# The first head's top-k mask from VectorE to ScalarE, for 27 of 36 query tiles

## The chip, the cores and the metric

One core of a Trainium2 chip runs one program. TensorE (PE in the rows) multiplies matrices, VectorE (DVE), ScalarE (ACT) and GpSimd (POOL) work elementwise, SyncE (SP) issues most DMAs. Each engine executes its own instructions in order and waits at semaphores for the others. The metric is the device time of one execution in microseconds (us).

## What is computed

Attention that keeps the 32 largest scores of each row, then a layer of four gated experts, then a layer that takes the largest of three products, all in float32:

```python
scores = scale * np.matmul(q, k.transpose(0, 1, 3, 2))     # 2 batches, 8 heads, 576 x 64
kth = np.partition(scores, -top_k, axis=-1)[..., -top_k:-top_k + 1]
mask = scores >= kth
scores = np.where(mask, scores, -1000000000.0)
attn = np.exp(scores - np.max(scores, axis=-1, keepdims=True))
attn = attn / (np.sum(attn, axis=-1, keepdims=True) + 1e-09)
x = np.matmul(attn, v)                                     # -> 1152 x 512
...
out += p[:, e:e + 1] * (np.maximum(x @ w1[e], 0.0) @ w2[e])      # 4 experts, 512 -> 1024 -> 512
...
h = np.maximum(np.maximum(x @ w1, x @ w2), x @ w3)               # 512 -> 768
return h @ w_out
```

## The kernel before, in words

**Units of work.** The 1152 rows are nine tiles of 128, in four chunks of 2, 2, 2 and 3 tiles. Attention runs over 36 *pairs*: a pair is one row tile and two heads, j = 0 (the first) and j = 1. Pairs are numbered from 0 here; the change concerns pairs 9 to 35. The layers after attention run by *phases*: experts of chunk 0, 1, 2, 3, then the last layer in three groups of tiles. The experts of a chunk need all of the chunk's attention. Each float32 product is three matmuls on split operands (high part and rest), at lines 606 to 608.

**One pair.** TensorE makes the scores (L368, bank `pss`), ScalarE copies them to `s` (L376). VectorE finds the 32 largest in seven steps, four of MAX8 (L389) and three of MATCH_REPLACE8 (L391), so that the last column of `m` is the 32nd largest, `kth`. ScalarE negates the maximum (`nb`, L396) and writes `p` = exp(SCALE s + nb) (L402). The *mask* then keeps of `p` what belongs to a score that is at least `kth`, and adds it up into `rs`: on VectorE one SCALAR_TENSOR_TENSOR with an accumulator (L409); the very first pairs do it on GpSimd. TensorE transposes the masked `p` (L427, and L432 for the last 64 columns of both heads), ScalarE copies that to `pt` (L430, L435), TensorE multiplies by v (`psv`, L469 and L472). On the side go the sum's guard (`rs`, L440), its reciprocal `rr` on VectorE (L446), its spreading `rb` on ScalarE (L450), a transpose `psr` (L455) and the copy `r` (L457); `xt` (L479) is the normalised tile.

**What sets the order.** The program is written out slot by slot, eight slots a pair. Each step of a pair stands at a fixed slot from the pair's first. For pairs 8 and later (table LOOSE) the second head runs 4 slots behind the first; the mask stands 7 slots after a head's first MAX8, the transposes 9 slots after it, their copies two slots later, the guard, reciprocal and spreading at slots 13, 14 and 15 of the pair, the product with v at 16. In between a planner puts the products of the layers (and the weight splits that they need, L229 and L235): it counts VectorE's work in a clock of its own (`dve`, 0.07 + n/960 us for n columns, a mask too) and TensorE's in another (`pe`), and after each slot issues products until TensorE's count has caught up with VectorE's.

```python
two(b0 + 7, pr.mask, j, lag=o["sum"] if n < EARLY else 3)
two(b0 + o["trans"], pr.trans_p, j)
...
clock["goal"] += (clock["dve"] - before) * SHARE[min(phase[0], len(SHARE) - 1)]
while clock["pe"] < clock["goal"]:
    if not advance():
```

The tiles of normalised attention are kept as `x`, in two sets that alternate between chunks. The `x` of chunk 3 takes the place of that of chunk 1, so it can only be written once the experts of chunk 1 are issued (`x_free`); tiles that come earlier wait in a list, `waiting`. After attention 48 pieces of the last layer's weights are converted (L200 to L212), and the remaining products follow.

Of the kernel before, what the change touches and what calls it, by code (L numbers as in the profile page):

```python
# [10 lines left out]
F32 = mybir.dt.float32  # L11
# [3 lines left out]
AF = mybir.ActivationFunctionType  # L15
# [11 lines left out]
PAUSE = 0.8  # L27
LATE = 3
ON_POOL = ((0, 1, 2, 3, 4, 5, 6, 7), (0, 1, 2, 3, 4, 5, 6))
W_FIRST, W_AHEAD = 60, 4  # L30
WIDE, W_FROM, W_STEP = 4, 306, 2

# [19 lines left out]
def kernel(  # L52
# [276 lines left out]
    def advance():  # L329

        return next(work, "end") not in (None, "end")
# [17 lines left out]
    class Pair:  # L349
        def __init__(self, n):  # L350
            self.c, self.hp, self.t = pairs[n]
            self.s, self.w, self.m, self.nb = {}, {}, {}, {}
            self.p = self.rs = None
            self.pt = {}

            self.did = set()

            self.on_pool = [n in ON_POOL[j] for j in range(2)]

        def scores(self, j):  # L360
            srcs = [(b, i) for i, (t, b) in enumerate(SLOTS[self.c]) if t == self.t]
# [36 lines left out]
        def exp(self, j):  # L398
            if self.p is None:
                self.p = at.tile([P, 2, S], F32, tag="p", name="p")  # L400
                self.rs = at.tile([P, 2], F32, tag="rs", bufs=3, name="rs")
            nc.scalar.activation(out=self.p[:, j].rearrange("p (a n) -> p a n", a=2), in_=self.s[j], func=AF.Exp, bias=self.nb[j], scale=SCALE)  # L402

        def mask(self, j):
            p = self.p[:, j].rearrange("p (a n) -> p a n", a=2)
            s, kth, total = self.s[j], self.m[j][:, TOPK - 1:TOPK], self.rs[:, j:j + 1]
            if not self.on_pool[j]:
                dve(S)
                nc.vector.scalar_tensor_tensor(out=p, in0=s, scalar=kth, in1=p, op0=ALU.is_ge, op1=ALU.mult, accum_out=total)  # L409
                self.did.update([("p", j), ("sum", j)])  # L410
                return lambda: None
            nc.gpsimd.tensor_scalar(out=s, in0=s, scalar1=kth, scalar2=None, op0=ALU.is_ge)
            nc.gpsimd.tensor_tensor(out=p, in0=p, in1=s, op=ALU.mult)  # L413
            self.did.add(("p", j))

            def add():
                nc.scalar.activation(out=s, in_=p, func=AF.Copy, accum_out=total)
                self.did.add(("sum", j))
            return add
# [74 lines left out]
    def attention():  # L494
# [34 lines left out]
        for n, (c, hp, t) in enumerate(pairs):  # L529
            s0 = 8 * n  # L530
            prs[n] = Pair(n)
            pr = prs[n]
            o = options(n)

            def two(s, f, *a, lag=o["lag"]):
                at_slot(s, lambda: at_slot(s + lag, f(*a)))
            for j in range(2):
                b0 = s0 + o["stag"] * j
                two(b0 + o["scores"], pr.scores, j)
                for i in range(7):  # L540
                    if o["new"]:
                        later.setdefault(b0 + i, []).insert(0, (pr.topk, (j, i)))
                    else:
                        at_slot(b0 + i, pr.topk, j, i)
                at_slot(b0 + 2, pr.negate, j)
                at_slot(b0 + 5, pr.exp, j)
                two(b0 + 7, pr.mask, j, lag=o["sum"] if n < EARLY else 3)
                two(b0 + o["trans"], pr.trans_p, j)
            two(s0 + o["stag"] + o["trans"], pr.trans_p, 2)
            at_slot(s0 + o["rec"] - 1, pr.guard)  # L550
            at_slot(s0 + o["rec"], pr.recip)
            at_slot(s0 + o["rec"] + 1, pr.spread)
            at_slot(s0 + o["pv"], pr.pv)
            two(s0 + o["rec"] + 2, pr.trans_r)
            end = max(o["pv"], o["rec"] + 2) + o["lag"]
            at_slot(s0 + end + 1, pr.norm)
            two(s0 + end + 2, pr.split_x)
# [282 lines left out]
    for s, done in attention():  # L840
        if s == GATES:
            load_gates()
        if s == GATES + 26:
            norm_gates()
        if s == W_FIRST - 12:
            w_load_to(3)
        if W_FIRST <= s < W_FIRST + 16 and not (s - W_FIRST) % 4:
            w_split_to((s - W_FIRST) // 4 + 1)
        if s == W_FROM - 6:
            for i in range(AHEAD_S):  # L850
                wide_load(i)
        if s >= W_FROM + W_STEP * conv and conv < WIDE * len(wide):
            converting.append(to_float32(conv))
            conv += 1
        for x in list(converting):
            if next(x, 0) == 0:
                converting.remove(x)
        split_waiting()
        assert not any((x.c, x.hp) in done for x in waiting)
        x_ready.update(done)  # L860
        clock["goal"] += (clock["dve"] - before) * SHARE[min(phase[0], len(SHARE) - 1)]
        before = clock["dve"]
        while clock["pe"] < clock["goal"]:
            if not advance():
                clock["pe"] = clock["goal"]
# [67 lines left out]
```

## Time and profile before

| | before |
|---|---|
| median of 3 runs | 778.3 us (776.51 to 778.96) |
| profiled execution, its own time | 778.73 us |
| its span on the engines | 776.9 us |
| TensorE / VectorE / ScalarE / GpSimd busy | 93% / 85% / 62% / 70% of the span |

The span runs from the first to the last instruction; the own time holds 1.8 us more around it. Busy shares are means over a program with three parts: attention alone (to about 100 us), attention with the experts' products in between (to about 471 us, when the last mask is done), and products with the conversion of weights. Durations of neighbouring matmuls overlap in the rows, so the price of one is the distance from its start to the next start, not its duration.

### The profile page before, as it was taken

How to read it: one execution, taken by the hardware profiler on the slowest of the kernel's cores; microseconds unless marked ns; L12 is line 12 of the kernel's file. 1: busy time of each engine (PE TensorE's matmuls, PEld its weight loads, DVE VectorE, ACT ScalarE, POOL GpSimd, SP SyncE). 2: the span in 40 equal slices, each digit the busy share in tenths (PEclk: the TensorE clock that was granted, in tenths of full speed). 3: DMA queues.
4: the chain of work that ended last, by engine and by line, in shares of the span. 5: the costliest groups of instructions: out<-in, count | busy, mean ns of one | idle time of the engine just before them, and what ended most of it. 6: DMA issues, size and time to landing. Idle time of an engine off the chain costs nothing. (4 is left out here: it accounts for less than half of the span.)

```text
span 776.9 us, 13519 instructions
## 1 busy us (share of the span) xinstructions
PE 725.2 (93%) x4646; PEld 655.3 (84%) x4646; DVE 659.9 (85%) x1247; ACT 482.3 (62%) x1021; POOL 541.4 (70%) x440
## 2 busy tenths in 40 slices
PE   3666799999999999998999998999999999999998
PEld 2545689988998988887998997989998799899996
DVE  6999999999999999999999996898899994243341
ACT  5666768767786876766777675655565643342441
POOL 3887988889998878778878695675677673343430
PEclk9986699999999999999999999999999999999999
DMA  4430255466645446263554454977667864362421
GB/s 117 105 111 1 60 147 162 137 179 163 195 142 177 126 148 180 87 180 107 150 145 137 137 163 153 301 233 250 221 215 260 252 204 136 102 211 92 156 91 40
DMA packets 48612, 119.91 MB, mean 154 GB/s; under 512 B 7840, under 2 KB 18080, under 8 KB 48544
## 3 DMA queue, kind: packets, MB, share of 16 engines
q1 hardware_dynamic: 40336, 110.40, 46.6%
q10 hardware_dynamic: 8208, 8.65, 3.2%
q8 instruction: 36, 0.59, 0.3%
q14 instruction: 32, 0.26, 0.1%
HBM read 110.38 MB, written 8.65 MB: 153 GB/s over the span
## 5 line engine op out<-in xcount | busy, mean ns | idle before, releaser
L235 POOL TENSOR_TENSOR wlo<-raw,whi 128x512 fp32r<-128x512 f32 x260 | 359.7, 1413 | 129.8 <-ACT whi L229 128.9
L229 ACT ACTIVATE whi<-raw 128x1024 fp32r<-128x1024 f32 x164 | 170.3, 1057 | 41.1 <-DMA raw<-in_w_dram 16.7
L389 DVE MAX8 m<-work 128x8 f32<-128x576 f32 x216 | 154.1, 739 | 0.1
L606 PE MATMUL ps<-xl,whi 128*128 128x256 f32 (+1 forms) x512 | 153.6, 300 | 0.0
L608 PE MATMUL ps<-xh,wlo 128*128 128x256 f32 (+1 forms) x512 | 151.3, 296 | 0.0
L607 PE MATMUL ps<-xh,whi 128*128 128x256 f32 (+1 forms) x512 | 151.2, 295 | 0.0
L235 DVE TENSOR_TENSOR wlo<-raw,whi 128x1024 fp32r<-128x1024 f32 x34 | 52.7, 1550 | 67.2 <-ACT whi L229 55.9
L391 DVE MATCH_REPLACE8 work<-m,work 128x576 f32<-128x576 f32 x144 | 106.0, 736 | 0.0
L607 PEld LDWEIGHTS ps<-xh,whi 128*128 128x128 f32 x512 | 97.2, 190 | 0.9
L606 PEld LDWEIGHTS ps<-xl,whi 128*128 128x128 f32 x512 | 97.1, 190 | 1.0
L608 PEld LDWEIGHTS ps<-xh,wlo 128*128 128x128 f32 x512 | 97.1, 190 | 0.0
L606 PE MATMUL ps<-wlo,h 128*128 128x512 f32 x192 | 77.6, 404 | 0.0
L608 PE MATMUL ps<-whi,h 128*128 128x512 f32 x192 | 75.4, 392 | 0.0
L607 PE MATMUL ps<-whi,h 128*128 128x512 f32 x192 | 75.3, 392 | 0.0
L409 DVE SCALAR_TENSOR_TENSOR p<-s,m,p 128x576 f32<-128x576 f32 x57 | 73.8, 1295 | 0.0
L608 PE MATMUL ps<-x2h,wlo 128*128 128x384 f32 x216 | 72.8, 337 | 0.0
L606 PE MATMUL ps<-x2l,whi 128*128 128x384 f32 x216 | 72.7, 337 | 0.0
L607 PE MATMUL ps<-x2h,whi 128*128 128x384 f32 x216 | 72.6, 336 | 0.0
L368 PE MATMUL pss<-kT,ql 128*128 128x288 f32 x160 | 54.7, 356 | 14.1 <-DVE ql L312 7.5
L212 POOL TENSOR_TENSOR narrow<-narrow,raw 128x256 int32<-128x256 int32 x48 | 40.3, 840 | 39.3 <-DVE narrow L209 10.5
L427 PE MATMUL psp<-ident,p 128*128 128x128 f32 x288 | 49.1, 298 | 17.8 <-POOL p L413 11.9
L427 PEld LDWEIGHTS psp<-ident,p 128*128 128x128 f32 x288 | 37.3, 153 | 24.4 <-POOL p L413 15.5
(97 smaller groups left out, 1632.6 us busy)
## 6 DMA issues: line engine op xcount, KB each, us to landing
raw<-in_w_dram SPq DMA_DIRECT2D x128, 512.0 KB, 3.7
raw<-narrow SPq DMA_DIRECT2D x36, 512.0 KB, 3.4
raw<-in_m_dram SPq DMA_DIRECT2D x36, 256.0 KB, 4.9
narrow<-narrow ACTq DMA_DIRECT2D x48, 128.0 KB, 4.4
kraw<-in_k_dram SPq DMA_DIRECT2D x14, 288.0 KB, 4.5
raw<-in_mo_dram SPq DMA_DIRECT2D x12, 256.0 KB, 4.3
out_dram<-ob ACTq DMA_DIRECT2D x9, 256.0 KB, 2.0
vt<-in_v_dram SPq DMA_DIRECT2D x8, 256.0 KB, 3.7
```

The lines of the kernel that those rows point to most:

```text
L212: nc.gpsimd.tensor_tensor(out=out.bitcast(I32), in0=out.bitcast(I32), in1=last, op=ALU.add)
L229: nc.scalar.activation(out=hi, in_=raw, func=AF.Copy)
L235: on.tensor_tensor(out=lo[:, x], in0=raw[:, x], in1=hi[:, x].bitcast(F32), op=ALU.subtract)
L368: nc.tensor.matmul(ps[:, 0:SH], lhsT=l, rhs=r, start=i == 0, stop=i == len(mm) - 1)
L389: nc.vector.max(m[:, 8 * r:8 * r + 8], src)
L391: nc.vector.match_replace(out=self.w[j], in_to_replace=m[:, 8 * r:8 * r + 8], in_values=src, imm_value=NEG)
L409: nc.vector.scalar_tensor_tensor(out=p, in0=s, scalar=kth, in1=p, op0=ALU.is_ge, op1=ALU.mult, accum_out=total)
L427: nc.tensor.transpose(ps[:, r * P:(r + 1) * P], self.p[:, part, part * TAIL + r * P:part * TAIL + (r + 1) * P], ident)
L606: nc.tensor.matmul(ps, lhsT=lh, rhs=rl, start=first, stop=False)
L607: nc.tensor.matmul(ps, lhsT=lh, rhs=rh, start=False, stop=False)
L608: nc.tensor.matmul(ps, lhsT=ll, rhs=rh, start=False, stop=last)
```

## The change

For head j = 0 of pairs 9 to 35 (27 masks) the mask goes from VectorE to ScalarE, as three activations. The first writes max(kth - s, 0) + 2^-100 min(kth - s, 0) over the scores `s` (a parametric ReLU). The second makes a bias of one column, `eb` = SCALE kth + nb. The third is exp(-SCALE 2^100 s + eb) into `p`, with the sum in its accumulator: a score below `kth` gives exp of a huge negative number, 0, and one that is at least `kth` gives exp(SCALE s + nb) as before. The old exponential of that head goes. The mask of these heads stands two slots later, and the transposes of the masked `p` three slots later. VectorE's count no longer holds these masks. Where the slots' end of a chunk finds a tile that still waits for `x`, products are now issued until it has its place.

```diff
+ON_ACT = (range(9, 36), ())
+STEEP = 2.0 ** 100
+MASK_LATE = 2
...
+            self.on_act = [n in ON_ACT[j] for j in range(2)]
...
-            nc.scalar.activation(out=self.p[:, j].rearrange("p (a n) -> p a n", a=2), in_=self.s[j], func=AF.Exp, bias=self.nb[j], scale=SCALE)
+            if not self.on_act[j]:
+                nc.scalar.activation(out=self.p[:, j].rearrange("p (a n) -> p a n", a=2), in_=self.s[j], func=AF.Exp, bias=self.nb[j], scale=SCALE)
...
+            if self.on_act[j]:
+                eb = at.tile([P, 1], F32, tag="eb%d" % j, name="eb")
+                nc.scalar.activation(out=s, in_=s, func=AF.Prelu, scale=-1.0, bias=kth, alpha=1.0 / STEEP)
+                nc.scalar.activation(out=eb, in_=kth, func=AF.Identity, scale=SCALE, bias=self.nb[j])
+                nc.scalar.activation(out=p, in_=s, func=AF.Exp, scale=-SCALE * STEEP, bias=eb, accum_out=total)
+                self.did.update([("p", j), ("sum", j)])
+                return lambda: None
...
-                two(b0 + 7, pr.mask, j, lag=o["sum"] if n < EARLY else 3)
-                two(b0 + o["trans"], pr.trans_p, j)
+                late = MASK_LATE * pr.on_act[j]
+                two(b0 + 7 + late, pr.mask, j, lag=o["sum"] if n < EARLY else 3)
+                two(b0 + o["trans"] + late + (late > 0), pr.trans_p, j)
...
-        assert not any((x.c, x.hp) in done for x in waiting)
+        while any((x.c, x.hp) in done for x in waiting):
+            assert advance()
+            clock["goal"] = max(clock["goal"], clock["pe"])
+            split_waiting()
```

How this stands in the built programs. VectorE, in the middle of attention, over about a pair, before (the two L409 rows are the masks of one head each):

```order
L409 SCALAR_TENSOR_TENSOR p,rs<-s,m_3192,p 128x576
L389 MAX m_3375<-s 128x8
L389 MAX m_3293<-work 128x8
L391 MATCH_REPLACE work<-m_3375,s 128x576
L391 MATCH_REPLACE work<-m_3293,work 128x576
L389 MAX m_3375<-work 128x8
L389 MAX m_3293<-work 128x8
L686 SCALAR_TENSOR_TENSOR h<-ps_3260,h 128x512
L391 MATCH_REPLACE work<-m_3375,work 128x576
L479 TENSOR_TENSOR xt<-psv,r 128x128
L409 SCALAR_TENSOR_TENSOR p,rs<-s,m_3293,p 128x576
```

The same half of a pair on VectorE in the changed program, whose lines are numbered 4 to 12 higher:

```order
L458 RECIPROCAL rr<-rs 128x2
L395 MATCH_REPLACE work<-m_3224,work 128x576
L393 MAX m_3313<-s 128x8
L393 MAX m_3224<-work 128x8
L395 MATCH_REPLACE work<-m_3313,s 128x576
L395 MATCH_REPLACE work<-m_3224,work 128x576
L393 MAX m_3313<-work 128x8
L393 MAX m_3224<-work 128x8
L395 MATCH_REPLACE work<-m_3313,work 128x576
L491 TENSOR_TENSOR xt<-psv,r 128x128
L421 SCALAR_TENSOR_TENSOR p,rs<-s,m_3224,p 128x576
```

After the reciprocal the search of the next head starts at once: only the second head's mask is left.

ScalarE at the same place, before: the tail of one pair (`rb`, two `pt`) runs into the exponentials of the next.

```order
L396 ACTIVATE nb<-m_3638 128x1
L376 ACTIVATE s<-pss 128x288 x2
L678 ACTIVATE h<-raw 128x512
L450 ACTIVATE rb<-rr 128x128
L430 ACTIVATE pt<-psp 128x512
L435 ACTIVATE pt_3666<-psp 128x128
L229 ACTIVATE whi<-raw 128x1024
L684 ACTIVATE h<-ps_3685 128x512
L402 ACTIVATE p<-s,nb 128x576
L396 ACTIVATE nb<-m_3750 128x1
```

And in the changed program:

```order
L442 ACTIVATE pt<-psp 128x512
L380 ACTIVATE s<-pss 128x288 x2
L232 ACTIVATE whi<-raw 128x1024
L697 ACTIVATE h<-ps_3567 128x512
L462 ACTIVATE rb<-rr 128x128
L442 ACTIVATE pt<-psp 128x512
L447 ACTIVATE pt_3609<-psp 128x128
L414 ACTIVATE s<-s,m_3482 128x576
L415 ACTIVATE eb<-m_3482,nb 128x1
L416 ACTIVATE p,rs<-s,eb 128x576
L407 ACTIVATE p<-s,nb 128x576
L232 ACTIVATE whi<-raw 128x1024
```

Three new activations stand in one block behind the copies of the pair before, and the first head's `pt` copy has moved down to just ahead of the second's.

TensorE around pair 28, from its last transposes to its product with v, in the changed program (matmuls of the layers between them left out):

```order
L439 MATMUL psp<-ident,p 128x128 x4
L372 MATMUL pss<-kT,ql 128x288
...
L439 MATMUL psp<-ident,p 128x128 x4
L444 MATMUL psp<-ident,p 128x128
L619 MATMUL ps_4627<-wlo,h 128x512
...
L621 MATMUL ps_4840<-xh,wlo 128x256
L481 MATMUL psv<-pt_4668,v_last_115 128x128
L484 MATMUL psv<-pt,vt 64x128 x8
```

In the dots after the L444 row stand 102 matmuls of the layers; at the same pair before there were 48. It is the place where the added loop issues products so that chunk 3 gets its `x`. By the last pair's transposes the program before has issued 1152 of the layers' matmuls of 256 columns and 534 of 512, the changed one 1104 and 516; the rest comes later.

## Rows read from the trace of the kernel before

**Rows 1.** page, part 1 (busy us, share, instructions) and TensorE's slices of part 2

```profile
PE 725.2 (93%) x4646; PEld 655.3 (84%) x4646; DVE 659.9 (85%) x1247; ACT 482.3 (62%) x1021; POOL 541.4 (70%) x440
...
PE   3666799999999999998999998999999999999998
```

**Rows 2.** busy time by stretch, to and from the last mask at 471

```profile
110.00:471.00 361.00, 352.77 (x2660) 318.85 (x2658) 360.38 (x743) 265.09 (x571) 304.30 (x241) 1.00 0.52 153
471.00:776.90 305.90, 300.66 (x1581) 277.23 (x1579) 196.46 (x282) 145.90 (x261) 155.87 (x128) 1.00 0.56 181
```

**Rows 3.** waits of VectorE, 110 to 471 us: total, times, longest

```profile
DVE rr L446 <- ACT rs L440: 0.3, 1, 0.3
```

**Rows 4.** matmuls by line and shape, 110 to 471 us

```profile
L606 PE MATMUL ps<-xl,whi 128*128 128x256 f32 x354 | 102.1, 288 | 0.0
...
L606 PE MATMUL ps<-wlo,h 128*128 128x512 f32 x178 | 72.1, 405 | 0.0
```

**Rows 5.** TensorE's timeline, neighbours of 256 and 512 columns: start, us

```profile
294.95 0.39 PE L608 MATMUL ps<-whi,h 128*128 128x512 f32 x1
295.18 0.40 PE L606 MATMUL ps<-wlo,h 128*128 128x512 f32 x1
...
303.03 0.28 PE L607 MATMUL ps<-xh,whi 128*128 128x256 f32 x1
303.15 0.28 PE L608 MATMUL ps<-xh,wlo 128*128 128x256 f32 x1
```

**Rows 6.** TensorE's timeline, an attention pair's own matmuls

```profile
311.24 0.29 PE L368 MATMUL pss<-kT,ql 128*128 128x288 f32 x1
311.37 0.29 PE L368 MATMUL pss<-kT,qh 128*128 128x288 f32 x1
...
313.17 0.60 PE L427 MATMUL psp<-ident,p 128*128 128x128 f32 x4
313.60 0.27 PE L432 MATMUL psp<-ident,p 128*128 128x128 f32 x1
...
316.48 0.38 PE L469 MATMUL psv<-pt,v_last 128*128 128x128 f32 x2
...
317.90 0.38 PE L368 MATMUL pss<-kT,ql 128*128 128x288 f32 x1
```

**Rows 7.** groups of instructions, whole span: busy us, mean ns of one

```profile
L402 ACT ACTIVATE p<-s,nb 128x576 f32<-128x576 f32 x72 | 55.7, 774 | 0.0
...
L409 DVE SCALAR_TENSOR_TENSOR p<-s,m,p 128x576 f32<-128x576 f32 x57 | 73.8, 1295 | 0.0
...
L396 ACT ACTIVATE nb<-m 128x1 f32<-128x1 f32 x72 | 14.0, 197 | 10.5 <-DVE m L389 10.3
...
L409 DVE DVE_READ_ACCUMULATOR p<-s,m,p 128x1 f32 x57 | 4.3, 76 | 0.0
...
L417 ACT ACTIVATION_READ_ACCUMULATOR s<-p 128x1 f32 x15 | 2.8, 187 | 0.0
...
L106 ACT ACT_TABLE_LOAD x1 | 1.3, 1283 | 0.7 <-PEq L912 0.7
```

**Rows 8.** line 409's durations: min/median/max ns, first and last start

```profile
L409 DVE SCALAR_TENSOR_TENSOR p<-s,m,p x57: 797/1321/1948, 92.0 to 469.5; 128x576 f32<-128x576 f32 x57
```

**Rows 9.** VectorE's timeline, two of these masks

```profile
309.42 1.29 DVE L409 SCALAR_TENSOR_TENSOR p<-s,m,p 128x576 f32<-128x576 f32 x1
...
315.53 0.80 DVE L409 SCALAR_TENSOR_TENSOR p<-s,m,p 128x576 f32<-128x576 f32 x1
```

**Rows 10.** GpSimd's timeline at these masks

```profile
308.80 3.08 POOL L235 TENSOR_TENSOR wlo<-raw,whi 128x512 fp32r<-128x512 f32 x2 [1.29 <-ACT whi L229]
...
317.57 5.67 POOL L235 TENSOR_TENSOR wlo<-raw,whi 128x512 fp32r<-128x512 f32 x4 [5.28 <-ACT whi L229]
```

**Rows 11.** waits of ScalarE, 110 to 471 us

```profile
ACT rb L450 <- DVE rr L446: 27.5, 20, 2.6
```

**Rows 12.** waits of TensorE, 110 to 471 us

```profile
PE psv L469 <- ACT pt L435: 3.5, 4, 1.6
```

## The prediction

> **What bounds the kernel now.** First the busy shares and the slices: TensorE is at 9 tenths or more in nearly every slice from a seventh of the span on, VectorE averages 85% [rows 1]. Two engines can be full at once, so the next view is the busy time by stretch. The change touches pairs 9 to 35, and these lie between 110 and 471 us. There VectorE is busy for 360.38 of 361.00 us, TensorE for 352.77, GpSimd for 304.30 and ScalarE for 265.09; behind 471 us TensorE has 300.66 of 305.90 and VectorE only 196.46 [rows 2]. The waits say which of the two paces attention: VectorE waited 0.3 us in 361, once [rows 3]. So attention runs as fast as VectorE does, and what follows runs as fast as TensorE does.
>
> The gain is not what VectorE saves. TensorE has a fixed amount of work, and from the first products to the end it is nearly always at it; the program can only become shorter by the time in which TensorE does nothing. How much is that between 110 and 471? Two bounds. What the busy time leaves open is 361.00 - 352.77 = 8.2 us [rows 2]; the ends of matmuls are modelled there, so short waits can hide. The other bound counts. There are 3 x 354 matmuls of the layers with 256 columns and 3 x 178 with 512 (lines 606, 607 and 608 alike) [rows 4]. Where nothing holds them up, their starts are 0.12 and 0.23 us apart [rows 5]: 1062 x 0.12 + 534 x 0.23 = 127.4 + 122.8 = 250.2 us. A pair's own matmuls: eight for the scores at 0.13 (1.04), eight transposes in two groups at 0.43 and the small one at 0.1 (0.96), the product with v and `psr` 317.90 - 316.48 = 1.42 [rows 6]; together 3.42, times 27 is 92.3. 361 - 250.2 - 92.3 = 18.5 us. This end is too high: four of the 27 pairs cover a tile with rows of both batches and take more. I take 12 us of idle, nearer to the end that is read directly, with 8.2 and 18.5 kept for the range.
>
> **The change part by part.**
>
> *VectorE.* 27 masks go, each 1.295 + 0.076 us with its accumulator read [rows 7]: 37.0 us. The mean hides two prices: the quickest mask took 0.797 us, the slowest 1.948 [rows 8]. The mask at 309.42 us took 1.29 us while GpSimd was in a subtraction; that at 315.53 took 0.80, and GpSimd stood idle then until 317.57 [rows 9, 10]. The removed masks stand where the kept ones do, so the mean holds for them too. If no GpSimd work met them, it would be 27 x 0.873 = 23.6 us. VectorE alone would end attention at 471 - 37.0 = 434 us (447 by the other price).
>
> *TensorE.* No matmul is added, but the planner lets products through as its count of VectorE's work grows, and that count loses the 27 masks. By the last pair's transposes the changed program has issued 48 fewer matmuls of 256 columns and 18 fewer of 512: 48 x 0.12 + 18 x 0.23 = 9.9 us [rows 5] that move behind attention, where TensorE is the pace. So the part behind attention grows from 305.9 to 315.8 us. TensorE's need up to there is 361 - 12 - 9.9 = 339.1 us; without any idle it would come to the last pair at 449.1 us. VectorE could be there at 434. TensorE becomes the pace of this part too, and 449.1 + 315.8 = 764.9 us is the least that the span can be with 12 us of idle at stake.
>
> *ScalarE.* The old exponential (0.774) is replaced by one with an accumulator (0.774, and 0.187 for the read), and there are two more: the parametric ReLU over the same 576 columns and a bias of one column. Neither occurs in the rows. The nearest to the first is the exponential, with a column as its bias as well, 0.774; a copy of one column takes 0.197 [rows 7]. Below, the ReLU can't be less than the 0.187 of a read; above, I allow the two 1.3 us together for their waits on each other, since each reads what the one ahead wrote. I take 0.774 + 0.197 + 0.187 = 1.16 us a mask, 31.3 us (between 15 and 40). 265.1 + 31.3 = 296.4 us in about 343 us is 86%, where it was 73%. This hides as long as ScalarE's waits shrink: it had 95.9 us without work [rows 2] and would have 47. 27.5 us of them were waits of `rb` for VectorE's reciprocal, 20 times [rows 11], and these go as VectorE stops being late.
>
> *Later mask, later transposes.* Two slots later for `p`, three for its transposes: the product with v is still at slot 16, so the first head's `pt` copy now stands right ahead of the second's. TensorE waits for these copies already, 3.5 us in 4 waits [rows 12]. Behind the waiting `psv` on TensorE stand `psr`, the next scores and products. The copies wait behind `rb`, which waits for VectorE; with VectorE ahead of TensorE this wait becomes shorter, while a fuller ScalarE makes it longer. I let these cancel.
>
> *The forced products.* At pair 28 TensorE gets 102 products in place of 48 ahead of the next pairs' scores: 54 x 0.23 = 12.4 us at most [rows 5]. TensorE is working in that time, so this costs it nothing. VectorE may stand still for as much, and its time for attention is then 434 + 12.4 = 446 us, still below 449. If the masks' price is the low one it is 459, ten past 449, and the span 459 + 315.8 = 774.8, the upper end of the forecast's own range.
>
> *Hidden.* GpSimd loses what TensorE's postponed products would have asked of it and gains nothing; the new `eb` tile and the longer life of `s` meet no reader on the path.
>
> **The sum.** 776.9 - 12 of TensorE's idle, + 4 us that stay: a third of the present, because TensorE and VectorE now want nearly the same time per pair (339 and 324 us for 27) and must meet several times in each. Span 768.9; with 1.8 around it 770.7. The profiled run's own time, 778.73, is 0.4 above the median, so the median would be 770.3: **770 us**, 1.1% less.
>
> **Rivals.**
>
> *A, the forecast:* TensorE paces attention, 8 to 18.5 us of idle less what stays: 761 to 775. Chance 0.63.
>
> *B, ScalarE becomes the pace, slower.* Its waits belong to its order and need not vanish: it stops at `rb`, `r`, `xt` and scores whatever its load, and a block of three activations (about 2 us) now stands ahead of the second head's exponential and the next score copies. If all 95.9 us stayed, attention would take 361 + 31.3 us and the program 110 + 392.3 + 315.8 = 818 us. It breaks even where attention ends at 461, which allows 351 - 296.4 = 54.6 us, 57% of the waits. With three quarters staying, 71.9 us, it is 110 + 368.3 + 315.8 = 794. For it: 86% load in strict order. Against it: VectorE's single wait of 0.3 us shows that ScalarE has been well ahead of it. Chance 0.20.
>
> *C, nothing to gain.* TensorE's idle is only the visible 8.2 us, and waits for late `pt` copies make up for them: 776 to 780. For it: those copies now come three in a row. Chance 0.15.
>
> *E, table switches.* ScalarE loaded its table once, 1.283 us [rows 7]; if the new functions asked for another table twice a mask, 54 x 1.283 = 69 us would be added to ScalarE, 365 us without a single wait, and the program would take at least 110 + 365 + 315.8 = 791 us. The changed program holds one load, at its start, as before, which speaks against it. Chance 0.02. The Trainium skill (ScalarE: Activation LUTs, Table sets: the hidden batching unit) advises to batch activations by table set and not by function. Its figure of about 2.66 us a switch would make 144 us of the 54. No row here shows a second load.
>
> **Range and chances.** Of A, 761 and above; upward it takes in all of C and the part of B that is near break-even: **761 to 783 us**, which leaves out nearly all the rest of B, E and a sliver of A below 761, 2 in 10 together. A alone: 761 to 775. Changes under 0.3%, 2.3 us, can't be told from none in this kernel. Faster by more (below 776): A and a little of C, 0.65. Within: most of C and B's edge, 0.15. Slower: 0.20.
>
> **What the changed profile would show.** Right: attention's last mask at about 453 us in place of 471; VectorE with tens of us of waits where it had 0.3, mostly for scores or products, one long one near pair 28; TensorE's busy time closer to its stretch; 27 parametric ReLUs near 0.77 us; ScalarE near 86% of attention, its wait at `rb` far below 27.5 us. Wrong: if TensorE waits for `psv` or `psp` more than now, with ScalarE as the releaser, B or C holds; if the last mask is at 471 or later, B. If VectorE still has no waits, its masks were worth less than 37 us, or TensorE's idle was larger than 12.

## The result: 785.98 us, slower by 1%

Four runs of the changed kernel took 785.28 to 788.04 us, median 785.98; the kernel before had 778.63 beside them. The ratio is 1.0100 [1.0067, 1.0133]: slower, outside the range of 761 to 783. The profiled execution took 785.28 us with a span of 783.5. The page of the changed kernel, where [rows 1] stood before:

```profile
PE 726.8 (93%) x4646; PEld 657.8 (84%) x4646; DVE 638.6 (82%) x1193; ACT 504.5 (64%) x1102; POOL 530.5 (68%) x440
...
PE   3665799999996999999999998999999999999998
```

TensorE has a 6 in a stretch that was full, the thirteenth slice (235 to 255 us). The second view is the end of attention. The last mask of VectorE (line 421; durations, then the starts of the first and the last of the two masks in the window):

```profile
L421 DVE SCALAR_TENSOR_TENSOR p<-s,m,p x2: 1482/1512/1541, 450.6 to 461.7; 128x576 f32<-128x576 f32 x2
```

It ends at 463.1 us. Before, it ended at 470.3 (the 471 of [rows 2] is the round end of a stretch), and the prediction had 453. The busy time on both sides of it, where [rows 2] stood before (span, then busy us of PE, PEld, DVE, ACT, POOL, granted clock, DMA share, GB/s):

```profile
110.00:463.10 353.10, 343.99 (x2600) 312.12 (x2598) 329.50 (x688) 282.69 (x646) 283.39 (x234) 0.99 0.51 149
463.10:783.50 320.40, 312.08 (x1650) 287.04 (x1650) 207.89 (x289) 151.50 (x269) 167.24 (x135) 0.99 0.56 181
```

VectorE, which had 0.6 us without work in its stretch, now has 23.6. But TensorE has not closed up: 9.1 us are open where 8.2 were. Behind the last mask the program takes 320.4 us, 4.6 more than the forecast 315.8. So the loss against the forecast has two parts, 10.1 us in attention and 4.6 behind it; together, but for rounding, the span's 783.5 against the forecast 768.9.

The new instructions on ScalarE, by group (busy us, mean ns of one):

```profile
L414 ACT ACTIVATE s<-s,m 128x576 f32<-128x576 f32 x27 | 21.2, 785 | 0.0
L416 ACT ACTIVATE p<-s,eb 128x576 f32<-128x576 f32 x27 | 21.0, 776 | 0.9
...
L415 ACT ACTIVATE eb<-m,nb 128x1 f32<-128x1 f32 x27 | 8.1, 300 | 0.0
...
L109 ACT ACT_TABLE_LOAD x1 | 1.3, 1283 | 0.7 <-PEq L928 0.7
```

A mask costs what was expected. In the timeline a block goes from its start at 296.65 to the next instruction at 298.45, 1.80 us, and the plain exponential behind it takes 0.67 to the next start: 1.13 us more a mask, where the prediction had 1.16. ScalarE's busy time rose by less than the 31.3 us of the prediction's sum, from 482.3 to 504.5 us, and it is busy for 282.69 of 353.10 us of attention, 80% where 86% was forecast.

```profile
296.65 0.81 ACT L414 ACTIVATE s<-s,m 128x576 f32<-128x576 f32 x1
...
298.45 0.76 ACT L407 ACTIVATE p<-s,nb 128x576 f32<-128x576 f32 x1
299.12 0.61 ACT L691 ACTIVATE h<-raw 128x512 fp32r<-128x512 f32 x1
```

So the waits, 110 to 463.1 us, of the changed kernel (total, times, longest):

```profile
ACT whi L232 <- DMA raw<-in_w_dram: 21.8, 13, 5.0
ACT rb L462 <- DVE rr L458: 12.9, 12, 2.2
DVE h L699 <- ACT h L697: 10.8, 8, 3.0
...
PE ps L619 <- ACT pt L442: 6.1, 1, 6.1
...
PE psv L481 <- ACT pt L447: 1.8, 4, 0.6
```

ScalarE's wait at `rb` fell as forecast, from 27.5 us [rows 11] to 12.9. A wait came up that the prediction has not: for weights (`raw`, converted to `whi` on ScalarE). Before, in the same view of 110 to 470 us:

```profile
ACT whi L229 <- DMA raw<-in_w_dram: 9.2, 13, 1.8
```

The two together were 36.7 us and are 34.7, so the time won at `rb` came back at the weights, in pieces of up to 5.0 us in place of 1.8. (All of ScalarE's time without work fell, from 95.9 us [rows 2] to 70.4, since its other waits became shorter too.) One of these pieces reaches TensorE. TensorE's timeline there:

```profile
237.85 0.27 PE L444 MATMUL psp<-ident,p 128*128 128x128 f32 x1
244.25 0.58 PE L619 MATMUL ps<-xl,whi 128*128 128x256 f32 x1 [6.12 <-ACT pt L442]
244.63 0.41 PE L620 MATMUL ps<-xh,whi 128*128 128x256 f32 x1
244.84 0.41 PE L621 MATMUL ps<-xh,wlo 128*128 128x256 f32 x1
...
248.21 0.28 PE L619 MATMUL ps<-xl,whi 128*128 128x256 f32 x1
248.32 0.28 PE L620 MATMUL ps<-xh,whi 128*128 128x256 f32 x1
```

TensorE waits 6.12 us for the copy to `pt`, which gives back the PSUM bank that `psp` holds. ScalarE stood elsewhere:

```profile
231.15 0.71 ACT L380 ACTIVATE s<-pss 128x288 f32<-128x288 f32 x2
235.27 1.06 ACT L232 ACTIVATE whi<-raw 128x1024 fp32r<-128x1024 f32 x1 [3.42 <-DMA raw<-in_w_dram]
...
242.07 1.06 ACT L232 ACTIVATE whi<-raw 128x1024 fp32r<-128x1024 f32 x1 [4.97 <-DMA raw<-in_w_dram]
...
243.61 0.59 ACT L442 ACTIVATE pt<-psp 128x512 f32<-128x512 f32 x1
```

Why the weight was late stands on two more engines. A weight takes one of three `raw` buffers, and the buffer comes back when GpSimd has made `wlo` of it; then SyncE may issue the next load. GpSimd, and then SyncE's queue:

```profile
224.12 1.86 POOL L315 TENSOR_TENSOR ql<-qraw,qh 128x768 fp32r<-128x768 f32 x1
226.06 2.83 POOL L274 TENSOR_TENSOR kT<-kraw,kT 64x576 fp32r<-64x576 f32 x2
228.97 5.08 POOL L238 TENSOR_TENSOR wlo<-raw,whi 128x512 fp32r<-128x512 f32 x4
```

```profile
231.56 0.33 SPq L183 DMA_DIRECT2D raw<-in_w_dram  x1
231.94 2.49 SPq L259 DMA_DIRECT2D qraw<-in_q_dram  x4
234.48 1.25 SPq L259 DMA_DIRECT2D kraw<-in_k_dram  x2
235.84 2.01 SPq L183 DMA_DIRECT2D raw<-in_w_dram  x2
```

GpSimd split q and the keys before it came to the weights, and the next loads of weights stood behind six loads of q and k in one queue, 3.9 us. The two waits of ScalarE differ in this. The load of the first weight was issued at 231.56, 0.03 us after its buffer came back, and landed 3.6 us later: no queue is in this wait, only GpSimd's late return. The second buffer came back at 234.05; its load was issued at 235.84, 1.8 us later, and took 6.2 us to land, where the median load takes 3.8. Before, GpSimd subtracted the two weights that give these buffers back (first row here, last row of GpSimd's above) ahead of the same splits:

```profile
222.34 5.04 POOL L235 TENSOR_TENSOR wlo<-raw,whi 128x512 fp32r<-128x512 f32 x4 [0.25 <-ACT whi L229]
227.33 1.85 POOL L312 TENSOR_TENSOR ql<-qraw,qh 128x768 fp32r<-128x768 f32 x1
229.14 3.08 POOL L235 TENSOR_TENSOR wlo<-raw,whi 128x512 fp32r<-128x512 f32 x2
232.30 2.83 POOL L271 TENSOR_TENSOR kT<-kraw,kT 64x576 fp32r<-64x576 f32 x2
```

So the first buffer came back at 224.87 there, 6.7 us earlier, and ScalarE was free for the weight at 230.20, 1.7 us earlier than the 231.85 of the changed kernel. At this place the weight came later; ScalarE did not come sooner.

And the wait has an aftermath: from 244.63 to 248.04 matmuls of 256 columns start 0.21 us apart and not 0.12 [rows 5], the granted clock is at its lower level, 1.2 GHz, for 6.8 us (it fell within the idle time), and 1.5 us more are lost by these spacings.

The second place is behind attention. TensorE:

```profile
481.57 0.39 PE L621 MATMUL ps<-whi,h 128*128 128x512 f32 x1
485.01 0.47 PE L619 MATMUL ps<-wlo,h 128*128 128x512 f32 x1 [3.05 <-ACT h L691]
...
487.50 0.63 PE L619 MATMUL ps<-wlo,h 128*128 128x512 f32 x1
487.93 0.63 PE L620 MATMUL ps<-whi,h 128*128 128x512 f32 x1
```

Here ScalarE, and then GpSimd:

```profile
483.20 0.36 ACTq L220 DMA_DIRECT2D narrow<-narrow  x1
483.61 0.60 ACT L690 ACTIVATE raw<-ps 128x512 f32<-128x512 f32 x1 [2.79 <-POOL narrow L215]
```

```profile
479.53 2.90 POOL L238 TENSOR_TENSOR wlo<-raw,whi 128x512 fp32r<-128x512 f32 x2
482.39 1.65 POOL L215 TENSOR_TENSOR narrow<-narrow,raw 128x256 int32<-128x256 int32 x2
```

The store of a converted piece stands in ScalarE's own queue, and waits for GpSimd's addition (L215), which stands behind a weight's subtraction. The activations behind the store wait with it, and TensorE for them. Then the matmuls of 512 columns start 0.43 us apart in place of 0.23 for 3.4 us. The granted clock by windows (last but two) falls at these two places alone behind the first eighth of the span; before, it fell nowhere there:

```profile
240.00:260.00 20.00, 15.75 (x115) 14.42 (x116) 16.42 (x33) 13.82 (x31) 11.94 (x10) 0.83 0.37 124
...
480.00:500.00 20.00, 16.38 (x76) 14.21 (x75) 16.41 (x21) 10.65 (x19) 15.36 (x14) 0.91 0.73 229
```

The Trainium skill (TensorE: Matmul & The Clock Gate, HAM oscillation) describes this aftermath: a TensorE that waits on loads comes back with a slow clock, so that a wait costs more than its length. The trace agrees: 6.1 us of wait and 1.5 behind it, 3.1 + 0.6 and 1.6 behind it. That is 12.9 us, to be set beside the 14.6 us by which the span is above the forecast (which allowed 4 us of open time in attention).

### The profile page after: what moved, and what is told of

It reads as the page before. It is cut to its first block, busy times and chain, and to the rows that moved or that the text cites. A ratio compares the mean times of both kernels' runs of the same rounds, so it can differ in the third digit from the quotient of the medians.

```text
span 783.5 us, 13551 instructions
## 1 busy us (share of the span) xinstructions
PE 726.8 (93%) x4646; PEld 657.8 (84%) x4646; DVE 638.6 (82%) x1193; ACT 504.5 (64%) x1102; POOL 530.5 (68%) x440
## 4 chain that ended last, share of the span: by engine, by line
PE 71%; DVE 13%; POOL 7%; issue 4%; ACT 3%; DMA 1%; SPq 0%; POOLq 0%; ACTq 0%
PE ps L619 19%; PE ps L621 19%; PE ps L620 19%; DVE m L393 6%; DVE work L395 5%; POOL wlo L238 5%; PE pss L372 3%; PE psv L484 3%; PE psp L439 2%; PE pso L620 2%; PE pso L619 2%; PE pso L621 2%; ACT whi L232 1%; PE psv L481 1%; DMA raw<-in_w_dram 1%
## 5 line engine op out<-in xcount | busy, mean ns | idle before, releaser
L238 POOL TENSOR_TENSOR wlo<-raw,whi 128x512 fp32r<-128x512 f32 x260 | 350.6, 1377 | 146.1 <-ACT whi L232 144.4
L619 PEld LDWEIGHTS ps<-xl,whi 128*128 128x128 f32 x512 | 98.7, 193 | 8.4 <-ACT pt L442 6.4
L372 PE MATMUL pss<-kT,ql 128*128 128x288 f32 x160 | 56.3, 366 | 14.0 <-DVE ql L315 7.5
L215 POOL TENSOR_TENSOR narrow<-narrow,raw 128x256 int32<-128x256 int32 x48 | 41.5, 866 | 34.5 <-DVE narrow L212 9.6
L439 PE MATMUL psp<-ident,p 128*128 128x128 f32 x288 | 48.8, 297 | 14.3 <-POOL p L425 12.9
L439 PEld LDWEIGHTS psp<-ident,p 128*128 128x128 f32 x288 | 37.5, 153 | 21.1 <-POOL p L425 16.4
L393 DVE MAX8 m<-s 128x8 f32<-128x576 f32 x72 | 53.9, 749 | 0.6 <-ACT s L380 0.6
```

Source lines behind the costliest of these rows:

```text
L215: nc.gpsimd.tensor_tensor(out=out.bitcast(I32), in0=out.bitcast(I32), in1=last, op=ALU.add)
L238: on.tensor_tensor(out=lo[:, x], in0=raw[:, x], in1=hi[:, x].bitcast(F32), op=ALU.subtract)
L372: nc.tensor.matmul(ps[:, 0:SH], lhsT=l, rhs=r, start=i == 0, stop=i == len(mm) - 1)
L393: nc.vector.max(m[:, 8 * r:8 * r + 8], src)
L439: nc.tensor.transpose(ps[:, r * P:(r + 1) * P], self.p[:, part, part * TAIL + r * P:part * TAIL + (r + 1) * P], ident)
L619: nc.tensor.matmul(ps, lhsT=lh, rhs=rl, start=first, stop=False)
```

## The experiments

Five theories were put against each other. **R**: weights come late, by the ring of three `raw` buffers and the one load queue. **S**: ScalarE's added work. **P**: the products that the planner postponed behind attention or forced at pair 28. **K**: the later transposes hold PSUM banks in a clump. **C**: the conversion of the last layer's weights, with its store in ScalarE's queue, makes the stall at 485 us. Times are medians, followed by the ratio to the kernel before and its 95% interval; "last mask" is where the last mask ends in the traced execution, "tail" the span behind it. All edits are to the changed kernel if not said otherwise.

**Is it ScalarE's load?** e3 puts a plain exponential with its sum in the three activations' place, so that nothing is masked in these heads and the output is wrong; e8 makes the change for every second pair only.

```diff
-                nc.scalar.activation(out=s, in_=s, func=AF.Prelu, scale=-1.0, bias=kth, alpha=1.0 / STEEP)
-                nc.scalar.activation(out=eb, in_=kth, func=AF.Identity, scale=SCALE, bias=self.nb[j])
-                nc.scalar.activation(out=p, in_=s, func=AF.Exp, scale=-SCALE * STEEP, bias=eb, accum_out=total)
+                nc.scalar.activation(out=p, in_=s, func=AF.Exp, bias=self.nb[j], scale=SCALE, accum_out=total)
```

> The changed kernel without the parametric ReLU and the bias of the 27 masks: one exponential with its sum stays at the late slot, and nothing is masked in these heads. ScalarE loses 27 x (0.78 + 0.29) = 29 us of work. S: the loss goes with it, 765 to 773. R: the queue of loads and the order are nearly the same, so late weights stay, 780 to 787, unless the shorter block lets ScalarE come to the weight splits sooner. P: 782 to 787.

782.84 us, 1.0035 [1.0019, 1.0052]; last mask 459.3. The work of 27 masks is gone from both engines, and the kernel is still slower than before: the stall is there (4.1 us, weights' longest wait 4.1), and so is that at 485 (3.1). S is worth 3 us of the 7 by the medians, 5 of 8 by the ratios, so ScalarE's added work is a good part of the loss: the stall at 244 is shorter without it. But neither stall needs it.

```diff
-ON_ACT = (range(9, 36), ())
+ON_ACT = (range(9, 36, 2), ())
```

> The change for every second pair from 9 on only (14 masks of 27). S: half the loss, 781 to 783. P (planner): half of the 9.9 us behind attention, 781 to 783. R and K: the loss is an accident of where loads, banks and weights meet, not a sum over masks, so it need not be halved: with another order the time is 768 to 776 if no stall of over 3 us occurs, and higher by such a stall and the lower clock behind it where one does.

785.36 us (779.7 to 787.2), 1.0085 [1.0058, 1.0113]. Half of the masks lose nearly as much as all, so the loss is not so much a mask. Its profiled execution, which took 780.37 us, has weights' waits of 6.8 us, none over 2.2; what the slower ones lost is not shown.

**Banks and the v load.** e5 has the transposes one slot earlier, e7 the load of v six slots later, since SyncE had waited 21.1 us at it (2.2 before).

```diff
-                two(b0 + o["trans"] + late + (late > 0), pr.trans_p, j)
+                two(b0 + o["trans"] + 2 * pr.on_act[j], pr.trans_p, j)
```

> The changed kernel with the first head's transposes one slot earlier (slot 11 in place of 12, still two behind the mask). Theory K (banks): at slots 12 and 13 five of the six PSUM banks now go out at once (first head's transposes, two for scores, second head's transposes and the small one), so TensorE's next product but one waits for the first head's copy whenever ScalarE is late; one slot earlier the copy is earlier too: the 6.1 us wait of a product for that copy at 244 us shrinks below 3, the lower clock behind it goes, 774 to 781. Theory R (late weights): ScalarE still stands 5 us at a weight, TensorE still stalls there, 783 to 788. Theory S (ScalarE's load): 783 to 788.

782.04 us, 1.0046 [1.0024, 1.0067]. In the traced execution (785.37 us, the longest of ten) TensorE's wait for a bank is gone, and one of 4.4 us for `pt` at the product with v stands in its place; weights are as late (19.4 us, longest 4.5). There K only chose at which instruction TensorE waits. The median is 4 us lower all the same, and what the other executions gained is not shown, so a share of K stays open.

```diff
-                at_slot(s0, load_v, *key[1:])
+                at_slot(s0 + 6, load_v, *key[1:])
```

> The changed kernel with each v load six slots later in the DMA queue. In the changed kernel the queue waits 21.1 us for the product with v that frees its buffer, with weights behind it (2.2 us before). R, if that wait is what makes weights late: ScalarE's waits for weights fall from 35.5 us to about 17 and the time to 772 to 778. If the six q and k loads ahead of the weight at 232 to 236 us make it late, the stall at 244 us stays: 781 to 787. K and S: 782 to 787.

786.46 us, 1.0099 [1.0071, 1.0127]: SyncE's wait at v is down to 3.3 us, and the stall keeps its 6.2 us. The v load is not the cause.

**Is the delay of two slots needed?** `MASK_LATE = 2` becomes 0.

> The changed kernel with mask and transposes of the first head at the slots they had before (7 and 9), on ScalarE still. K: no product waits for a first head's copy, 770 to 778. R: the weight that comes late still holds ScalarE for 3 to 5 us and TensorE stalls, by another bank, 780 to 787. S: ScalarE now waits for the 32nd largest as well, 787 or more.

799.41 us, 1.0273 [1.0236, 1.0310]. TensorE waits 16.9 us in 14 places for `pt` at the product with v, against 1.8 us with the delay. The delay is needed.

**The planner.** e4 counts the masks on ScalarE as if VectorE still did them, so that products keep their old places.

```diff
             if self.on_act[j]:
+                dve(S)
```

> The changed kernel, but the planner goes on counting the 27 masks as VectorE's work, so that TensorE's products stand where they stood before: nothing postponed, nothing forced at pair 28. P: 770 or less, as the 9.9 us come back under attention. S: 780 or more, attention slower. R: depends on where the q, k and v loads fall against the weights; a time under 776 only if ScalarE's longest wait for a weight is under 3 us.

777.98 us, 0.9974 [0.9963, 0.9985]: last mask 470.0, tail 306.3, the old numbers. It shows that the longer tail is postponed work. With the products at their old places VectorE's free time is worth 0.3%, while weights still come late: ScalarE's waits for them are 16.0 us, the longest 4.0, where the kernel before had 9.2 and 1.8. In e15 the q and k loads (see e12) are two slots earlier as well.

> The changed kernel with its masks still in the planner's count (as in e4, 778.0) and LOAD 13. Under R, the one stall of 3.2 us and the 3.4 us at the lower clock that e4 had left go as well: 773 to 776, last mask near 465. If that stall at 366 us has nothing to do with the weights' queue, it stays at 777 to 779.

779.64 us, 1.0024 [1.0005, 1.0042], a miss: e4's stall of 2.9 us at 366 is still there (2.8 at 370). In e4 it follows ScalarE's wait of 4.0 us for a weight whose load was issued 0.02 us after its buffer came back, so an earlier place in the queue had nothing to give there.

**Late weights.** e1 gives the weights a fourth `raw` buffer; its memory comes from the buffers that the scores and, later, the conversion use. e2 is the same on the kernel before.

```diff
-AHEAD_S = 5
+AHEAD_S = 4
...
-            raw = wp.tile([P, 1024], F32, tag="raw", bufs=3, name="raw")
+            raw = wp.tile([P, 1024], F32, tag="raw", bufs=4, name="raw")
```

> The changed kernel with four buffers for incoming weights in place of three, and four score and conversion buffers in place of five to make room. Theory R (late weights): the changed kernel loses about 15 us in two places, 244 and 485 us, where ScalarE stands at a weight that has not landed, TensorE runs out of free PSUM or operands for 6 and 4 us and then gets the lower clock for 7 and 3 us; a fourth buffer lets the load go out earlier, so ScalarE's waits for weights fall from 35.5 us to under 15, and the time to 768 to 774. Theory S (ScalarE's load): three more activations in strict order cost by themselves; the time stays at 782 to 787. Theory P (planner): the 9.9 us of products that moved behind attention and the forced products are the loss; 782 to 787.

> The kernel before with the same buffers (four for weights, four for scores and conversions): the control. R: its ScalarE waits for weights were short (16.7 us in all), so 775 to 779. S and P say the same.

e1: 801.92 us, 1.0245 [1.0175, 1.0315] by the three shorter of its four executions; e2: 805.13, 1.0313 [1.0261, 1.0364]. The price is paid at the end, by both (e2's tail is 335.9 us, where 306 was). But e1's last mask is at 454.2 us, with weights' waits of 1.1 us in all, in the trace of the longest, 807.2 us; e2's is at 467.7. R is right for attention; the kernel as a whole says nothing yet.

e12 takes a part of R: q and k loads two slots earlier, out of the way of the late weight.

```diff
-LOAD = 11
+LOAD = 13
```

> The changed kernel with the q and k loads two slots earlier in the DMA queue. R with the queue as cause (six loads of q and k stand ahead of the weight that comes late): the wait of 5 us for a weight at 237 us goes or moves, 776 to 781 if it goes. R with GpSimd as cause: the stall stays, 783 to 788.

783.34 us, 1.0052 [1.0029, 1.0075]. The one stall of 6.1 becomes two of 2.2 and 2.0, the lower clock lasts 3.4 us in place of 6.8, the longest wait for a weight is 3.1. The order of the queue is a part of it.

GpSimd's share was tried by giving the keys' subtraction to VectorE, in e10 for all pairs (`sub=nc.vector.tensor_tensor` as the default of `split_k`), in e11 with e9's edit too, in e16 from pair 9 on.

```diff
-            at_slot(at, split, *key[1:])
+            at_slot(at, split, *key[1:], *(((0, 1), nc.vector.tensor_tensor) if key[0] == "k" and n >= 9 else ()))
```

> The changed kernel with the subtraction that splits k on VectorE in place of GpSimd for all pairs (14 instructions of about 1.42 us on GpSimd become 0.76 us each on VectorE, which has time now). Theory R as it stands: weights come late because GpSimd gives their three buffers back late, ahead of the pile-up at 244 us by 2.8 us of k's split. GpSimd freed of it: ScalarE's waits for weights in attention fall from 21.8 us to under 14, no stall over 3 us at 244, last mask at 453 to 457 us, time 776 to 780 (the stall at 485 stays). If the q and k loads in the queue are what makes weights late, the stall stays: 783 to 788. S: 783 to 788.

> The last two edits together. R and C together hold the whole loss: last mask at 453 to 457, no stall over 2 us from 110 us on, 769 to 774, faster than the kernel before. If ScalarE's load or the planner's postponed products cost by themselves (S, P), 778 or more.

> The changed kernel with the k split on VectorE for pairs 9 and later alone (e10 without its loss before pair 9). If GpSimd's backlog (the k subtraction of 2.8 us ahead of the weights' subtraction) is what gives the raw buffers back late, the 6.1 us stall at 244 falls under 3 us, ScalarE's longest wait for a weight under 3.5 us, last mask near 458, and the median is 780 to 782 (the stall at 485 stays). If it is the order of the load queue alone, the stall keeps 5 to 6 us and the median 784 to 788.

803.65, 796.90 and 791.78 us (ratios 1.0319, 1.0244 and 1.0175). In e10 and e11 pair 9 comes 12 us later already, so they say little of this question. In e16 the weights' waits halve (10.4 us, longest 3.7) and the stall at 244 shrinks to one of 2.7 at 240.5, as R by GpSimd has it; but a split took 1.30 us in the mean on VectorE, not the 0.76 expected, ScalarE waits for VectorE at `rb` again (23.3 us) and TensorE 10.3 us for `pt` behind that, so the time is no verdict. What GpSimd's order and the queue's order add to the late weights in general stays open; for the two in front of the stall at 244 the trace told it above.

**The conversion.** e9 starts it 8 slots later.

```diff
-WIDE, W_FROM, W_STEP = 4, 306, 2
+WIDE, W_FROM, W_STEP = 4, 314, 2
```

> The changed kernel with the conversion of the last layer's weights starting 8 slots later (314 in place of 306). Theory C (conversions): behind attention the changed kernel is still in the experts of chunk 2, whose weights are all subtracted on GpSimd, when the conversions begin; ScalarE's queue stops at the store of a converted piece, which waits for GpSimd's addition, and TensorE stalls 3.2 us at 485 us, then 3.4 us at the lower clock, about 5 us in all. Later conversions: no stall there, 780 to 782. The stall at 244 us stays. If the 485 us stall has another cause, 784 to 788.

781.51 us, 1.0040 [1.0017, 1.0063]: the stall at 485 is gone, the tail 314.8 in place of 320.4, and the other stall keeps 5.5 us. C alone was moved by the edit: on all engines the two programs have the same instructions in the same order up to 467 us. The last mask is at 466.2 in this trace all the same, and not at 463.1; it has a wait of 1.58 us and 3.4 us at the lower clock near 217 us that the other trace lacks. So much can differ from one execution to the next.

**Both at once.** e13 joins e9 and e12, e14 does the same to the kernel before.

> The changed kernel with both edits that each took one of the two stalls smaller: conversion of the last layer's weights 8 slots later (W_FROM 314) and the q and k loads 2 slots earlier (LOAD 13). If the two stalls and the lower clock behind them are the whole loss (R and C together), both gains add: after 786.0 less 4.5 for the conversion less 2.6 for the load, with last mask near 460.5 and the tail near 315, so span 775 to 776 and a median near 777, and no TensorE stall above 3 us. If the lost time has another source (S or P), the gains overlap and it stays at 780 to 784.

> Control: the kernel before with the same two edits (W_FROM 314, LOAD 13). Its trace has neither stall, so under R and C it has nothing to gain: 777 to 780, last mask near 470, and e13 comes out level with it or up to 3 us ahead. If these edits are worth something for any kernel, it falls to 772 to 775 too and e13 says nothing about the change.

e13: 778.91 us, 1.0001 [0.9982, 1.0020]; e14: 778.03, 0.9999 [0.9980, 1.0017]. The gains add, and the kernel before gets nothing. e13's tail is 315.9 us, the forecast's; its last mask at 462.7 is not, with weights' waits of 18.2 us still. So e17 takes R away as e1 did, without e1's price: the two narrow pieces that give up their buffers use the place of `pt`, which attention no longer needs by then, and the second head's scores keep three buffers of five. e18 makes the same edits in the kernel before, as a control.

```diff
-WIDE, W_FROM, W_STEP = 4, 306, 2
+WIDE, W_FROM, W_STEP = 4, 314, 2
...
-            raw = wp.tile([P, 1024], F32, tag="raw", bufs=3, name="raw")
+            raw = wp.tile([P, 1024], F32, tag="raw", bufs=4, name="raw")
...
-        out = at.tile([P, 1024 // WIDE], F32, tag="s1", bufs=AHEAD_S, name="narrow")
+        out = at.tile([P, 1024 // WIDE], F32, tag=("s1", "s1", "s1", "pt0", "pt1")[n % 5], bufs=3 if n % 5 < 3 else 1, name="narrow")
...
-            s = at.tile([P, 2, SH], F32, tag="s%d" % j, bufs=AHEAD_S, name="s")
+            s = at.tile([P, 2, SH], F32, tag="s%d" % j, bufs=3 if j else AHEAD_S, name="s")
```

> The changed kernel with a fourth buffer for raw weights, this time without taking a buffer from the conversion of the last layer (two of its five narrow pieces use the place of the attention's pt instead), and with the conversion 8 slots later (W_FROM 314, as in e9). If late weights and the conversion (R and C) are what kept the forecast from coming true, both stalls are gone: last mask at 453 to 456 us, no TensorE stall near 244, ScalarE's longest wait for a weight under 2 us, tail 315 to 316, span 769 to 772 and median 770 to 773, which is the forecast's 770. If the postponed products or ScalarE's load (P, S) cost something of their own, or e1's early attention came from its smaller conversion buffers, the last mask is at 460 or later and the median 776 or above, as in e13 (778.9).

> Control: the kernel before with the same edits as e17. VectorE paces its attention, and ScalarE's longest wait for a weight was 1.8 us there, so R gives it little: last mask 467 to 470 (e2 had 467.7), tail 306, median 775 to 779. If it comes down as far as e17 does (770 to 773), the buffer is a gain of its own and not what the change lacked.

e17: **770.92 us** (769.18 to 773.92), 0.9914 [0.9883, 0.9945] of the kernel before. e18: 776.78, 0.9989 [0.9966, 1.0011], the kernel before as it was. e17's last mask, stretches and waits (110 to 470 us), from the trace of an execution of 769.42 us:

```profile
L421 DVE SCALAR_TENSOR_TENSOR p<-s,m,p x2: 1481/1510/1539, 440.5 to 451.6; 128x576 f32<-128x576 f32 x2
```

```profile
110.00:454.00 344.00, 341.24 (x2595) 309.72 (x2593) 324.20 (x685) 282.87 (x647) 282.53 (x234) 1.00 0.51 156
454.00:767.60 313.60, 309.21 (x1645) 285.55 (x1645) 209.04 (x286) 151.25 (x267) 166.03 (x134) 1.00 0.56 180
```

```profile
ACT rb L462 <- DVE rr L458: 14.8, 14, 1.7
...
PE psv L481 <- ACT pt L447: 2.1, 3, 0.8
ACT whi L232 <- DMA raw<-in_w_dram: 0.8, 2, 0.5
```

The last mask is done at 453.0 us (forecast 453), 314.6 us follow (forecast 315.8), the span is 767.6 (768.9), TensorE's open time in attention 2.8 us (4). Weights' waits went from 21.8 us to 0.8, and the wait at `rb` is 14.8 where it was 12.9.

## Why the prediction was wrong

**What held.** TensorE, not VectorE, sets the pace once the masks are gone; VectorE's 37.0 us are worth only TensorE's idle time. In e17 TensorE is at work 341.24 of 344.00 us, and the gain, 0.9%, is near the 1.1% that was worked out; e17 has a fourth buffer that the predicted kernel lacks, but the kernel before gains nothing by it (e18). The 9.9 us of postponed products show in the tail: 314.6 to 315.9 us where nothing stalls (e9, e13, e17), 306.3 where the planner counts the masks again (e4). The products forced at pair 28 cost TensorE nothing: it was at work for 20.00 of the 20 us from 360 to 380, while VectorE was for 12.14. ScalarE's price was 1.13 us a mask for 1.16, made up otherwise: `eb` took 300 ns and not the 197 of `nb`. The Trainium skill (ScalarE: Activation LUTs, Rules for kernel authors) puts an activation with a column as its bias at about 0.3 us and more by the element; `eb` has such a bias, and the trace agrees. Rival E is out: the table was loaded once, and no row here shows a switch. Rival B, ScalarE as the pace, is out too: ScalarE has 70.4 us without work in attention, its added work taken away (e3) leaves the stalls, if shorter ones, and its work kept (e17) allows the forecast.

**The step that failed** is in the part on later mask and transposes: "I let these cancel", with the "+ 4 us that stay" in the sum. ScalarE's freed wait at `rb` was taken as room. But ScalarE's order holds more waits than that one, and the part on what is hidden named GpSimd's work without its product: the `raw` buffers that it gives back, and the loads that wait for them. Before, a weight was at most 1.8 us late for ScalarE; now it is up to 5.0 us late, and ScalarE waits for it in front of TensorE's `pt`. That cost 10.1 us of attention (last mask 463.1, and 453.0 in e17; e9, with the same instructions in the same order on all four engines as e17 and other buffers alone, has 466.2). That the ring of three buffers is the reason is shown by e17 and e18. Why it no longer sufficed has two sources, and how they share is not shown. One is a ScalarE that is held up less: with the products at their old places (e4) the waits for weights rise from 9.2 to 16.0 us. The other is the new order of GpSimd's and SyncE's work once products are postponed: at the stall at 244 us the buffer came back 6.7 us later than before, and ScalarE was not early.

**The second miss** is a missing term. The tail was taken as the old one plus 9.9 us. But the postponed products meet the start of the conversion, and there ScalarE stopped at a store of its own queue. That cost 4.6 us above the forecast, 5.6 by e9; e4, which postpones nothing, has no such stall. (The sums of the prediction come out. Two of its readings were off by little: attention ended at 470.3 and not at 471, and ScalarE's busy time rose by 22.2 us and not by 31.3.)

The rival on the other side (B) had the right engine in its "stops at `rb`, `r`, `xt` and scores whatever its load" and the wrong releaser: it charged the stops to ScalarE's load and priced them at 794 us. Rival C named what TensorE would wait for, a late `pt` copy, but by three copies in a row: those waits, at `psv`, fell from 3.5 us [rows 12] to 1.8, and the 6.1 us at the other `pt` come from a weight. A row of 9.2 us of waits for weights stood in the trace of before, and the prediction did not read it.

## What to carry to other kernels

When an engine is relieved, list every wait of the engines that were held up by it, the short ones too, and ask for each how long its supply takes when nobody is late any more, and which work of the supplier now comes first: rings of buffers and load queues that just sufficed may no longer. A queue that an engine shares with stores can stop it for work that is in no hurry; here it was enough to start that work 8 slots later. And an experiment that gives one buffer should not take it from a place that is needed: e1 hid in its total what e17 showed.

## What the runs showed of the hardware

TensorE's granted clock fell to its lower level, 1.2 GHz, after single waits: 6.8 us of it at a wait of 6.12 us, 3.4 us at one of 3.05, and 3.4 us in e12 behind a wait of 2.21 us, but none behind its wait of 2.02 us, 8.7 us later. Shorter waits did it in one execution and not in another. A wait of 1.58 us at 217 us was followed by 3.4 us at the lower level in e9 and by none in e13. Two waits at the end of attention, 1.46 and 0.80 us long, left the clock up in the kernel before; nearly the same two, 1.47 and 0.80 us, were followed by 6.8 us at the lower level in e18. In the profiled execution of e17, with no wait over 1.0 us in that part, it did not fall from 100 us to the end.
